# A written order for the first steps of an attention and MoE kernel, with three sums of the second product at once

## The chip, the cores and the metric

The kernel runs on one core of one Trainium2 chip. Its engines work side by side and wait for each other by semaphores: TensorE (PE) for matrix products, ScalarE (ACT), VectorE (DVE), GpSimd (POOL), and SyncE (SP), whose queue issues the loads. The metric is the time of one execution on the device in microseconds (us); lower is better.

## The reference

Attention at two resolutions for 2 batches and 8 heads of 576 positions with 64 dimensions, then two feed-forward blocks over the 1152 tokens:

```python
q_d, k_d, v_d = (means of 4 neighbouring positions of q, k, v)
out_up = np.repeat(softmax(q_d @ k_d.T * scale) @ v_d, 4, axis=2)
mask = np.abs(pos[:, None] - pos[None, :]) < 4
out_local = softmax(np.where(mask, q @ k.T * scale, -1e9)) @ v
x = (out_up + out_local)                      # tokens x 512
h = x @ w_in;  x = (h / (1 + np.exp(-h))) @ w_out        # 512 -> 2048 -> 512
p = domain_probs / (domain_probs.sum(-1, keepdims=True) + 1e-9)
out = sum(p[:, e:e+1] * (np.maximum(x @ w1[e], 0) @ w2[e]) for e in range(4))
```

## The kernel before

Products run as fp32r, each operand split in a high and a low part: high times high, high times low, low times high. So `mm3` (line 538) issues three matmuls for a product.

**Attention in jobs.** A job (line 494) is one batch, one pair of heads (`hp`) and one part `c` of the positions: 256 positions in four blocks of 64 for c = 0, 320 in five for c = 1. Jobs 0 to 3 are batch 0, c = 0; jobs 4 to 7 batch 0, c = 1; jobs 8 to 15 the same for batch 1 (the second batch). A job's steps are: `load_kq`, `load_vg`, `load_vw`; `local_scores` on PE (S below, 361); `local_max` on DVE (x, 378); `local_exp` on ACT (e, 385); pooled k and q (`pool_kq`, 314; for jobs 0 to 3 `pool_kq_first`, 328, where PE sums k with an identity); `down_scores` on PE (D, 392); `down_max` (n on DVE, d on ACT, 404); `local_sum` (u, 389); `norm` (r on DVE, g on ACT, 412); `trans` (T on PE, its evacuation a on ACT, 424); `values` (V on PE, o on ACT, f on DVE, 451); `split_x` (h on ACT, l on DVE, 473), which leaves the high and low part of the tokens in `xh`, `xl`. The last 64 positions of a batch's pooled scores are taken in one tail step (tp on POOL, tD and tT on PE).

**First feed-forward block.** Its 2048 columns are done in two halves (`hf`), each over four chunks of tokens (`ci`: 256, 320, 256, 320; in the second half 256, 256, 256, 384). Chunk 0 is jobs 0 to 3, chunk 1 jobs 4 to 7. For a chunk the first product (`g1_step`, 573; G below) makes eight blocks `ft` of 128 columns out of four `k`; `g1_evac` (556) makes x times sigmoid of it (th on ACT, gf on DVE) and splits it into `gh` (ACT) and `gl` (DVE). The second product (`g2_step`, 590; H below) sums over the eight blocks f for each of four blocks `db` of outputs. Of chunk 0 the first three blocks of G are summed job by job while the attention runs (`start_mm`, 828; M0 to M3). PSUM holds three tiles for these products (line 67).

**Weights.** They come as 64-bit pieces of 512 KB: pieces 0 to 7 are the first 1024 columns of w_in, 8 to 15 the matching rows of w_out. `split_raw` (197) turns a piece into a high part and a low part: two ACT steps (L208, L209; A below), one DVE step (L210; C), the copy to the high part on ACT (L217; w) and the low part on POOL (L218; L). Six pieces can be held (three `stg` buffers, three places in `acc`); their decoded form `dec` has two buffers.

**What sets the order.** The tile scheduler orders each engine by priorities, which `at_tick`, `attn_tick` and `prio` set, and by dependencies that `follow` adds within an engine without a semaphore. Each engine works through its list in order; on SP a load also waits until the load eight places before it has landed. `FIRST_LOADS` (120) sets the first loads by name.

Of the kernel before, what the change touches and what calls it, by code (L numbers as in the profile page):

```python
# [21 lines left out]
HP = NH // 2  # L22
# [34 lines left out]
STAGE = 4  # L57
EXPERT = 72
# [3 lines left out]
def attention_moe_kernel(ctx, tc, kqa, kqb, qtl, va, vb, w64, w1d, w2d, dpr, out):  # L62
# [57 lines left out]
    FIRST_LOADS = ("kq0", "kq1", "vg0", "vw0", "kq2", "vg1", "vw1", "kq3", "vg2", "vw2", "vg3", "vw3",  # L120
                   "s0", "s1", "s2", "s3", "kq4", "s4", "s5", "kq5")
# [75 lines left out]
    def split_raw(u, j, t):  # L197
# [3 lines left out]
        if u < 8:  # L201
# [10 lines left out]
            key = (u, j) if u < 2 else u  # L212
            if key in behind_job:
                for a in (first, low):
                    follow(a, behind_job[key][0], "first weights")
                follow(i, behind_job[key][1], "first weights")
            ACT.activation(out=h[:, c], in_=d, func=ACTF.Copy)  # L217
            POOL.tensor_tensor(out=l[:, c], in0=d, in1=h[:, c].bitcast(F32), op=ALU.subtract)  # L218
# [20 lines left out]
    def constants():  # L239
# [38 lines left out]
    def load_vw(j):  # L278
# [26 lines left out]
    def padd(o, a, b):  # L305
        POOL.tensor_tensor(out=o, in0=a, in1=b, op=ALU.add)  # L306
# [54 lines left out]
    def local_scores(j):  # L361
# [4 lines left out]
        for m in range(nb):  # L366
            for h in range(2):
# [5 lines left out]
                else:  # L373
                    after(i, first[h])
        j.group = PE.matmul(out=j.ps[:, 0:nb * WIN], lhsT=ident16, rhs=mk.rearrange("p m c -> p (m c)"),
                            start=False, stop=True, skip_group_check=True)

    def local_max(j):
# [3 lines left out]
        DVE.tensor_reduce(out=j.st[:, 0:nb], in_=j.lo, axis=AX.X, op=ALU.max)  # L382
        DVE.tensor_tensor(out=j.lo, in0=j.lo, in1=j.st[:, 0:nb].unsqueeze(2).to_broadcast([128, nb, WIN]), op=ALU.subtract)

    def local_exp(j):
        p = j.ps[:, 0:j.nb * WIN]
        ACT.activation(out=p, in_=p, func=ACTF.Exp, scale=SC_L)

    def local_sum(j):
        DVE.tensor_reduce(out=j.ps[:, 496:496 + j.nb], in_=j.lo, axis=AX.X, op=ALU.add)  # L390

    def down_scores(j):
        i = PE.matmul(out=j.ps[:, 352:352 + SD], lhsT=j.qd.rearrange("p a b -> p (a b)"), rhs=kd[j.b, j.hp],
                      start=True, stop=True)
        after(i, j.group)
# [631 lines left out]
```

## Time and profile before

| | |
|---|---|
| runs | 667.74, 667.77, 672.28 us; median 667.77 |
| profiled execution | 669.87 us; span from first to last instruction 667.6 us |
| busy in the span | PE 96%, DVE 63%, ACT 50%, POOL 37% |
| granted clock of PE, mean over the span | 0.986 |

A row of the busy table gives each engine's busy time in a stretch with its number of instructions. In the rows by time the first number is the start in us from the span's start, the second the time from the first start to the last end of the group, x the number of instructions; in brackets stands the idle time before and what ended it.

### The profile page before, as it was taken

The page shows a single profiled execution, that of the slowest core. Times are in us where ns is not written, and L with a number is a line of the kernel's source. Part 1 is how long each engine was busy: PE and PEld are TensorE (multiplying, and loading weights), DVE is VectorE, ACT ScalarE, POOL GpSimd, SP SyncE. Part 2 cuts the span into 40 slices and gives each one's busy share as a digit, 9 for nine tenths or more (in the row PEclk, how much of TensorE's full clock was granted, in tenths as well). Part 3 has the DMA queues.
Part 4 walks back from the last instruction along what each step waited for, and adds up shares of the span by engine and source line. Part 5 has one row for each costly group of instructions (what it writes and reads, how often), then busy time and mean ns, then how long its engine had stood idle before and what let it go on. Part 6 is the DMA issues. An engine that isn't in the chain of part 4 may idle for free.

```text
span 667.6 us, 13740 instructions
## 1 busy us (share of the span) xinstructions
PE 642.5 (96%) x5516; PEld 626.6 (94%) x5516; DVE 418.4 (63%) x851; ACT 330.5 (50%) x753; POOL 245.5 (37%) x346
## 2 busy tenths in 40 slices
PE   4879999999999999999999999999999999999995
PEld 4758988999999999999999999999999999999995
DVE  3569676475634644766467975568954769765444
ACT  2888765477843543454335643346533356433321
POOL 5546741114510000642356433456422654433210
PEclk9598999999999999999999999999999999999999
DMA  8975622007410400140002310012300020000001
GB/s 233 348 223 165 211 86 63 16 11 227 152 64 1 127 1 1 64 159 1 1 1 71 123 61 2 1 33 96 99 29 1 1 65 1 1 32 33 2 32 48
DMA packets 16927, 48.16 MB, mean 72 GB/s; under 512 B 2976, under 2 KB 4256, under 8 KB 16864
## 3 DMA queue, kind: packets, MB, share of 16 engines
q1 hardware_dynamic: 16864, 47.29, 22.3%
q8 instruction: 43, 0.70, 0.4%
q14 instruction: 20, 0.16, 0.1%
HBM read 44.93 MB, written 2.36 MB: 71 GB/s over the span
## 4 chain that ended last, share of the span: by engine, by line
PE 82%; DMA 6%; ACT 4%; DVE 4%; POOL 3%; issue 1%; SPq 0%; POOLq 0%; ACTq 0%; DVEq 0%
PE mm L540 52%; PE p L759 26%; DMA stg<-in_w_dram 3%; DMA vg<-in_va_dram 2%; DMA vg_f<-in_va_dram 1%; DVE gl L566 1%; DVE dec L210 1%; PE s L369 1%; ACT stg L209 1%; POOL wbuf L218 1%; PE t L432 1%; ACT dec L208 1%; PE o L464 1%; DVE acc L787 1%; POOL kq L306 1%
## 5 line engine op out<-in xcount | busy, mean ns | idle before, releaser
L540 PE MATMUL mm<-xh,wbuf 128*128 128x256 f32 (+2 forms) x1280 | 265.0, 294 | 5.4 <-DVE gf L560 3.5
L540 PEld LDWEIGHTS mm<-xh,wbuf 128*128 128x128 f32 x1280 | 208.9, 189 | 7.7 <-DVE gf L560 5.0
L540 PE MATMUL mm<-xl,wbuf 128*128 128x256 f32 (+2 forms) x640 | 187.7, 294 | 0.0
L741 POOL TENSOR_TENSOR r<-r 128x128 f32<-128x128 f32 x160 | 95.1, 607 | 177.8 <-ACT r L735 133.4
L744 DVE TENSOR_TENSOR h<-r,h 128x384 fp32r<-128x384 f32 (+1 forms) x128 | 91.8, 719 | 64.2 <-ACT h L743 64.0
L540 PEld LDWEIGHTS mm<-xl,wbuf 128*128 128x128 f32 x640 | 121.0, 189 | 0.2
L743 ACT ACTIVATE h<-r 128x384 fp32r<-128x384 f32 (+1 forms) x128 | 73.6, 578 | 93.3 <-POOL r L741 54.2
L540 PE MATMUL mm<-gh,wbuf 128*128 128x256 f32 (+2 forms) x512 | 102.6, 295 | 0.2 <-ACT acc L600 0.2
L759 PE MATMUL p<-wext,h 128*128 128x256 f32 x672 | 89.4, 276 | 0.0
L759 PE MATMUL p<-wbuf,h 128*128 128x256 f32 x672 | 82.7, 276 | 0.0
L540 PEld LDWEIGHTS mm<-gh,wbuf 128*128 128x128 f32 x512 | 81.9, 188 | 0.7 <-ACT acc L600 0.4
L759 PEld LDWEIGHTS p<-wext,h 128*128 128x128 f32 x672 | 82.4, 188 | 0.0
L759 PEld LDWEIGHTS p<-wbuf,h 128*128 128x128 f32 x672 | 79.4, 188 | 0.0
L540 PE MATMUL mm<-gl,wbuf 128*128 128x256 f32 (+2 forms) x256 | 74.0, 294 | 0.0
L741 DVE TENSOR_TENSOR r<-r 128x128 f32<-128x128 f32 x96 | 39.3, 409 | 35.6 <-ACT r L735 31.2
L735 ACT ACTIVATE r<-mm 128x512 f32<-128x512 f32 x48 | 28.6, 596 | 65.4 <-PE mm L540 65.0
L566 DVE TENSOR_TENSOR gl<-gf,gh 128x256 fp32r<-128x256 f32 (+2 forms) x64 | 39.0, 612 | 19.7 <-ACT gh L565 18.8
L540 PEld LDWEIGHTS mm<-gl,wbuf 128*128 128x128 f32 x256 | 47.8, 188 | 0.1
L218 POOL TENSOR_TENSOR wbuf<-dec,wbuf 128x512 fp32r<-128x512 f32 x24 | 32.1, 1354 | 25.9 <-ACT wbuf L217 19.8
L684 POOL TENSOR_TENSOR wext<-kst,wext 128x512 fp32r<-128x512 f32 x8 | 10.4, 1298 | 77.0 <-ACT wext L682 42.6
L560 DVE SCALAR_TENSOR_TENSOR gf<-th,mm 128x256 f32<-128x256 f32 (+2 forms) x64 | 28.4, 450 | 16.4 <-ACT th L559 15.1
L787 DVE SCALAR_TENSOR_TENSOR acc<-p,pr,acc 128x256 f32<-128x256 f32 (+1 forms) x63 | 36.1, 604 | 3.6 <-PE p L759 3.0
(138 smaller groups left out, 932.1 us busy)
## 6 DMA issues: line engine op xcount, KB each, us to landing
stg<-in_w_dram SPq DMA_DIRECT2D x25, 512.0 KB
kst<-in_w2d_dram SPq DMA_DIRECT2D x16, 512.0 KB
kst<-in_w1d_dram SPq DMA_DIRECT2D x12, 512.0 KB
acc<-in_w_dram SPq DMA_DIRECT2D x7, 512.0 KB
kq<-in_kqb_dram SPq DMA_DIRECT2D x8, 323.0 KB
kq<-in_kqa_dram SPq DMA_DIRECT2D x6, 419.0 KB
stg<-in_w1d_dram SPq DMA_DIRECT2D x4, 512.0 KB
vw<-in_vb_dram SPq DMA_DIRECT2D x8, 180.0 KB
```

The lines of the kernel that those rows point to most:

```text
L208: first = ACT.activation(out=d, in_=v[:, :, 1].bitcast(F32), func=ACTF.Prelu, scale=2.0 ** -112, alpha=2.0 ** 32)
L218: POOL.tensor_tensor(out=l[:, c], in0=d, in1=h[:, c].bitcast(F32), op=ALU.subtract)
L540: ins = [PE.matmul(out=ps, lhsT=l, rhs=r, start=(first and i == 0), stop=(last and i == n - 1)) for i, (l, r) in enumerate(pairs)]
L560: DVE.scalar_tensor_tensor(out=gf[:, 0:n], in0=th[:, 0:n], scalar=1.0, in1=ps[:, 0:n], op0=ALU.add, op1=ALU.mult)
L566: latest[DVE] = DVE.tensor_tensor(out=gl[ft][:, 0:n], in0=gf[:, 0:n], in1=gh[ft][:, 0:n].bitcast(F32), op=ALU.subtract)
L684: b = eng.tensor_tensor(out=l[:, r], in0=x, in1=h[:, r].bitcast(F32), op=ALU.subtract)
L735: ACT.activation(out=r[:, 0:4].rearrange("p s t -> p (s t)"), in_=ps[:, 0:512], func=ACTF.Relu)
L741: latest[eng] = eng.tensor_tensor(out=r[:, o], in0=r[:, a], in1=r[:, b], op=op)
L743: ACT.activation(out=h, in_=r[:, part], func=ACTF.Copy)
L744: latest[DVE] = DVE.tensor_tensor(out=l, in0=r[:, part], in1=h.bitcast(F32), op=ALU.subtract)
L759: ins = [PE.matmul(out=ps, lhsT=x, rhs=y, start=(opens and k == 0 and i == 0), stop=(k == 3 and i == n - 1), skip_group_check=True) for i, ...
L787: DVE.scalar_tensor_tensor(out=o, in0=ps, scalar=p, in1=o, op0=ALU.mult, op1=ALU.add)
```

## The change

The loads, and every step of the first eight jobs, of chunk 0 and of chunk 1's first product get a name by `mark`; the table `WRITTEN` lists the names engine by engine (one list each for SP, PE, ACT, DVE and POOL), and `written` ties each to the one before with `follow`. The ticks of jobs 0 to 3 stand closer. Other edits: k of jobs 0 to 3 is pooled by one DVE reduction in place of four PE products and an ACT copy; for pieces 0, 3, 9 and 13 the second of the two ACT steps is a shift on DVE (B below), for pieces 3 and 4 the copy to the high part is DVE's; `qdl` is zeroed by ACT at the start; in chunk 0 of the first half the second product runs three sums side by side, with f as the outer loop.

```diff
+LOW_ON_DVE = (0, 3, 9, 13)
+WHI_ON_DVE = (3, 4)
...
-    FIRST_LOADS = ("kq0", "kq1", "vg0", "vw0", "kq2", "vg1", "vw1", "kq3", "vg2", "vw2", "vg3", "vw3",
-                   "s0", "s1", "s2", "s3", "kq4", "s4", "s5", "kq5")
+    FIRST_LOADS = ("kq0", "kq1", "vg0", "vw0", "s0", "kq2", "vg1", "vw1", "s1", "kq3", "vw2", "vg2", "vg3", "s2",
+                   "vw3", "s3", "s4", "s5", "kq4", "s6", "vw4", "s7", "s8", "kq5", "s9", "qt", "vw5", "s10", "s11",
+                   "kq6", "s12", "kq7", "s13", "s14", "s15", "vw6", "vw7")
...
+    def mark(name, *ins):
+        steps.setdefault(name, []).extend(ins)
+        return ins[-1]
+
+    def written(names):
+        ins = [i for n in names.split() for i in steps[n]]
+        for a, i in zip(ins, ins[1:]):
+            follow(i, a, "written order")
...
-            low = ACT.activation(out=v[:, :, 0], in_=top, func=ACTF.Copy, scale=2.0 ** -13, bias=2.0 ** -14 - 0.5)
+            if 4 * u + j in LOW_ON_DVE:
+                low = mark(f"B{4 * u + j}", DVE.tensor_scalar(out=v[:, :, 0], in0=v[:, :, 0], scalar1=29, scalar2=None,
+                                                              op0=ALU.logical_shift_right))
+            else:
+                low = mark(f"A{4 * u + j}", ACT.activation(out=v[:, :, 0], in_=top, func=ACTF.Copy, scale=2.0 ** -13,
+                                                           bias=2.0 ** -14 - 0.5))
...
-            ACT.activation(out=h[:, c], in_=d, func=ACTF.Copy)
-            POOL.tensor_tensor(out=l[:, c], in0=d, in1=h[:, c].bitcast(F32), op=ALU.subtract)
+            if 4 * u + j in WHI_ON_DVE:
+                mark(f"w{4 * u + j}", DVE.tensor_copy(out=h[:, c], in_=d))
+            else:
+                mark(f"w{4 * u + j}", ACT.activation(out=h[:, c], in_=d, func=ACTF.Copy))
+            mark(f"L{4 * u + j}", POOL.tensor_tensor(out=l[:, c], in0=d, in1=h[:, c].bitcast(F32), op=ALU.subtract))
...
-        for r in range(4):
-            i = PE.matmul(out=kp, lhsT=ident, rhs=k4[:, :, r], start=(r == 0), stop=(r == 3))
-            if r == 0:
-                after(i, j.group)
-        ACT.activation(out=kd[j.b, j.hp], in_=kp, func=ACTF.Copy)
+        mark(f"k{j.i}", DVE.tensor_reduce(out=kd[j.b, j.hp], in_=k4, axis=AX.X, op=ALU.add))
...
-                    t = FIRST + PER * k
+                    t = FIRST + (PER if k > 3 else 2) * k
...
-    def g2_step(u0, hf, db, o, n):
+    def g2_step(u0, hf, dbs, o, n):
         c = slice(o, o + n)
-        ps = mm_tile()
+        sums = [(d, mm_tile()) for d in dbs]
         for f in range(8):
-            wh, wl = unit[u0 + f // 4]
...
+            for db, ps in sums:
+                g2_product(u0, db, f, ps, n)
+        for db, ps in sums:
+            g2_evac(hf, db, c, ps, n)
...
+    WRITTEN = (
+        """in_kq0 in_kq1 in_vg0 in_vw0 in_s0 in_kq2 in_vg1 in_vw1 in_s1 in_kq3 in_vw2 in_vg2 in_vg3 in_s2 in_vw3
...
+        """S0 S1 D0 D1 S2 T0 S3 T1 V0 D2 D3 V1 M0 T2 V2 M1 T3 S4 V3 M2 D4 S5 M3 tD G0_3_0 G0_3_1 D5 G0_3_2 G0_3_3
...
+        """tab e0 e1 A0 d0 d1 w0 g0 g1 A1 a0 w1 e2 e3 o0 a1 d2 h0 d3 A2 g2 o1 A3 h1 w2 a2 g3 A4 o2 A5 a3 h2 A6 e4
...
             for db in range(4):
                 next_step(dt)
-                g2_step(u0 + 2, hf, db, o, n)
+                if (hf, ci) != (0, 0):
+                    g2_step(u0 + 2, hf, [db], o, n)
+                elif db in (0, 3):
+                    g2_step(u0 + 2, hf, range(3) if db == 0 else range(3, 4), o, n)
```

The first loads on SP, at the program's start, in the kernel before (`stg` and `acc<-in_w` are pieces of weights, `kq` k and q of a job, `vg` and `vw` its v):

```order
L128 DMA kq<-in_kqa_dram 128x838 x2
L128 DMA vg_f_158<-in_va_dram 72x1024
L128 DMA vw<-in_va_dram 72x512
L128 DMA kq_f<-in_kqa_dram 128x838
L128 DMA vg_f_200<-in_va_dram 72x1024
L128 DMA vw<-in_va_dram 72x512
L128 DMA acc<-in_kqa_dram 128x838
L128 DMA vg_f_279<-in_va_dram 72x1024
L128 DMA vw_f_284<-in_va_dram 72x512
L128 DMA vg_f_376<-in_va_dram 72x1024
L128 DMA vw_f_381<-in_va_dram 72x512
L128 DMA stg_135<-in_w_dram 128x512
```

The same place in the changed kernel:

```order
L131 DMA kq<-in_kqa_dram 128x838 x2
L131 DMA vg_f_156<-in_va_dram 72x1024
L131 DMA vw<-in_va_dram 72x512
L131 DMA stg_137<-in_w_dram 128x512
L131 DMA kq_f<-in_kqa_dram 128x838
L131 DMA vg_f_186<-in_va_dram 72x1024
L131 DMA vw<-in_va_dram 72x512
L131 DMA stg_231<-in_w_dram 128x512
L131 DMA acc<-in_kqa_dram 128x838
```

The first piece of weights has moved from behind the loads of four jobs to the fifth place, the second to the ninth.

ACT's first steps before (`dec<-stg` and `stg<-stg` are A, `wbuf<-dec` is w, `kd<-s` the copy of pooled k, `s<-s` e, `ed,s<-` d, `ed<-ed` g, `at` and `atd` a):

```order
L336 ACTIVATE kd<-s 128x144
L387 ACTIVATE s<-s 128x280
L336 ACTIVATE kd<-s 128x144
L387 ACTIVATE s<-s 128x280
L409 ACTIVATE ed,s<-s,st 128x144 x2
L420 ACTIVATE ed<-ed,st 128x144
L208 ACTIVATE dec<-stg_135 128x512
L209 ACTIVATE stg_135<-stg_135 128x512
L208 ACTIVATE dec<-stg_211 128x512
L209 ACTIVATE stg_211<-stg_211 128x512
L420 ACTIVATE ed<-ed,st 128x144
```

And in the changed kernel:

```order
L410 ACTIVATE s<-s 128x280 x2
L222 ACTIVATE dec<-stg_137 128x512
L433 ACTIVATE ed,s<-s,st 128x144 x2
L239 ACTIVATE wbuf<-dec 128x512
L445 ACTIVATE ed<-ed,st 128x144 x2
L222 ACTIVATE dec<-stg_231 128x512
L228 ACTIVATE stg_231<-stg_231 128x512
L458 ACTIVATE at<-t_233 70x512
L465 ACTIVATE atd_243<-t_234 72x256
L239 ACTIVATE wbuf<-dec 128x512
```

The first two pieces now stand among the exponentials and scalings of jobs 0 and 1, and the copies of pooled k are gone.

On PE, the second product of chunk 0 where the middle blocks of f are used, in the changed kernel (`gh_642` and `gl_641` are f = 2, `gh_640` and `gl_639` f = 3; o is V of job 6):

```order
L565 MATMUL mm<-gh_642,wbuf 128x256 x2
L565 MATMUL mm<-gl_641,wbuf 128x256
L565 MATMUL mm<-gh_642,wbuf 128x256
L565 MATMUL mm<-gh_640,wbuf 128x256
L565 MATMUL mm<-gl_639,wbuf 128x256
L565 MATMUL mm<-gh_640,wbuf 128x256
L483 MATMUL o<-atd_587,vd 64x80 x4
L487 MATMUL o<-at,vw 64x64 x10
L565 MATMUL mm<-gh_640,wbuf 128x256
L565 MATMUL mm<-gl_639,wbuf 128x256
```

Each f is used by three sums before the next f; before, the scheduler put four or five f of one sum in a row.

## Rows read from the trace of the kernel before

**Rows 1.** The page's first part: busy us (share of the span) and instructions.
```profile
PE 642.5 (96%) x5516; PEld 626.6 (94%) x5516; DVE 418.4 (63%) x851; ACT 330.5 (50%) x753; POOL 245.5 (37%) x346
```

**Rows 2.** Busy time by stretches: stretch, its length, engines; granted clock, DMA share.
```profile
core 0: us, PE busy (x) PEld busy (x) DVE busy (x) ACT busy (x) POOL busy (x), PEclk, DMA share, GB/s
20.00:25.00 5.00, 4.12 (x47) 2.83 (x44) 3.01 (x6) 4.95 (x11) 0.84 (x1) 0.50 1.03 407
...
20.00:75.00 55.00, 48.42 (x523) 41.74 (x520) 42.30 (x100) 48.68 (x126) 29.90 (x37) 0.87 0.70 235
...
85.00:667.60 582.60, 573.76 (x4810) 566.74 (x4808) 365.27 (x721) 270.75 (x599) 198.03 (x273) 1.00 0.15 48
```

**Rows 3.** TensorE in order of time: start us, us, [idle before <-releaser].
```profile
31.31 0.61 PE L540 MATMUL mm<-xh,wbuf 128*128 128x256 f32 x3
...
50.60 0.38 PE L540 MATMUL mm<-xh,wbuf 128*128 128x256 f32 x1 [2.77 <-DVE gf L560]
...
82.67 0.50 PE L460 MATMUL o<-atd,vd 72*64 72x80 f32 x8
82.96 0.79 PE L464 MATMUL o<-at,vw 70*64 70x64 f32 x20
```

**Rows 4.** Loads issued on SP, and ACT's first step on weights, by time.
```profile
8.35 0.30 SPq L128 DMA_DIRECT2D vw_f<-in_va_dram  x1
...
9.84 0.35 SPq L128 DMA_DIRECT2D stg<-in_w_dram  x1
...
12.09 0.33 SPq L128 DMA_DIRECT2D stg<-in_w_dram  x1
...
19.45 0.66 ACT L208 ACTIVATE dec<-stg 128x512 f32<-128x512 f32 x1 [1.61 <-DMA stg<-in_w_dram]
```

**Rows 5.** TensorE at a granted clock of 0.50: transposes, then scores.
```profile
18.33 1.06 PE L432 MATMUL t<-ident,sm 128*70 128x128 f32 x4
...
20.80 1.20 PE L369 MATMUL s<-acc 64*64 64x70 f32 x16
```

**Rows 6.** ACT in order of time: an interval between two starts prices the first.
```profile
39.25 0.59 ACT L435 ACTIVATE at<-t 70x512 f32<-70x512 f32 x1 [0.39 <-PE t L432]
39.74 0.37 ACT L442 ACTIVATE atd<-t 72x256 f32<-72x256 f32 x1
40.01 0.38 ACT L476 ACTIVATE xh<-o 128x256 fp32r<-128x256 f32 x1
40.27 1.26 ACT L208 ACTIVATE dec<-stg 128x512 f32<-128x512 f32 x2
41.44 1.23 ACT L209 ACTIVATE stg<-stg 128x512 int32<-128x512 uint16 x2
42.56 0.37 ACT L409 ACTIVATE ed<-s,st 128x144 f32<-128x144 f32 x1
...
43.40 1.15 ACT L217 ACTIVATE wbuf<-dec 128x512 fp32r<-128x512 f32 x2
44.44 0.38 ACT L476 ACTIVATE xh<-o 128x256 fp32r<-128x256 f32 x1
```

**Rows 7.** VectorE and GpSimd in order of time, by start.
```profile
32.03 1.31 DVE L210 SCALAR_TENSOR_TENSOR dec<-dec,acc 128x512 int32<-128x512 int32 x2
...
53.13 3.54 DVE L566 TENSOR_TENSOR gl<-gf,gh 128x256 fp32r<-128x256 f32 x2
...
53.30 2.52 POOL L218 TENSOR_TENSOR wbuf<-dec,wbuf 128x512 fp32r<-128x512 f32 x2
```

**Rows 8.** TensorE in order of time, full clock: scores of the second batch, products.
```profile
70.54 0.71 PE L369 MATMUL s<-kq 64*64 64x70 f32 x16
...
72.28 0.39 PE L540 MATMUL mm<-gh,wbuf 128*128 128x256 f32 x1
...
78.53 0.39 PE L540 MATMUL mm<-gh,wbuf 128*128 128x256 f32 x2
...
80.91 0.41 PE L393 MATMUL s<-kd,qbd 128*128 128x144 f32 x2
```

More of the change, by code (lines that the diff above doesn't have):

```diff
@@ L208, in split_raw @@
             first = ACT.activation(out=d, in_=v[:, :, 1].bitcast(F32), func=ACTF.Prelu, scale=2.0 ** -112, alpha=2.0 ** 32)
-            low = ACT.activation(out=v[:, :, 0], in_=top, func=ACTF.Copy, scale=2.0 ** -13, bias=2.0 ** -14 - 0.5)
+            mark(f"A{4 * u + j}", first)
+            if 4 * u + j in LOW_ON_DVE:
[4 more added lines that the diff above has]
+                                                           bias=2.0 ** -14 - 0.5))
             i = DVE.scalar_tensor_tensor(out=ai, in0=ai, scalar=3, in1=v[:, :, 0],
                                          op0=ALU.logical_shift_left, op1=ALU.bitwise_or)
[L212 to L216, printed above, removed]
-            ACT.activation(out=h[:, c], in_=d, func=ACTF.Copy)
-            POOL.tensor_tensor(out=l[:, c], in0=d, in1=h[:, c].bitcast(F32), op=ALU.subtract)
+            mark(f"C{4 * u + j}", i)
+            if 4 * u + j == 16:
+                for a, b in ((first, "gh0_7"), (low, "gh0_7"), (i, "gl0_7")):
+                    follow(a, steps[b][-1], "written order")
+            if 4 * u + j in WHI_ON_DVE:
[3 more added lines that the diff above has]
+            mark(f"L{4 * u + j}", POOL.tensor_tensor(out=l[:, c], in0=d, in1=h[:, c].bitcast(F32), op=ALU.subtract))
         else:
@@ L252, in constants @@
             POOL.memset(t, 0.0)
-        POOL.memset(qdl, 0.0)
+        z = ac.tile([128, 1], F32, name="zero")
+        DVE.memset(z, 0.0)
+        mark("tab", ACT.activation(out=qdl.rearrange("p a b c -> p (a b c)"), in_=z.to_broadcast([128, HP * 32]), func=ACTF.Copy))
     class Job:
-        pass
+        i = None
     kd, vd, atd = {}, {}, {}
@@ L285, in load_vw @@
         else:
-            last_load.append(SP.dma_start(out=j.vw, in_=vb[j.b, j.hp]))
+            last_load.append(load(f"vw{j.i}", j.vw, vb[j.b, j.hp]))
     def load_vg(j):
@@ L305, in padd @@
     def padd(o, a, b):
-        POOL.tensor_tensor(out=o, in0=a, in1=b, op=ALU.add)
+        return POOL.tensor_tensor(out=o, in0=a, in1=b, op=ALU.add)
     def pmul(o, a, b):
@@ L340, in pool_kq_first @@
             p = slice(64 * h, 64 * h + 64)
-            DVE.tensor_reduce(out=j.qd[p, h], in_=q4[p], axis=AX.X, op=ALU.add)
+            mark(f"q{j.i}", DVE.tensor_reduce(out=j.qd[p, h], in_=q4[p], axis=AX.X, op=ALU.add))
     def pool_v(j):
@@ L414, in norm @@
         sums = j.ps[:, 496:497 + nb]
-        DVE.tensor_scalar(out=sums, in0=sums, scalar1=1e-9, scalar2=None, op0=ALU.add)
-        DVE.reciprocal(out=j.st[:, 13:14 + nb], in_=sums)
+        mark(f"r{j.i}", DVE.tensor_scalar(out=sums, in0=sums, scalar1=1e-9, scalar2=None, op0=ALU.add),
+             DVE.reciprocal(out=j.st[:, 13:14 + nb], in_=sums))
         if nb:
@@ L419, in norm @@
             i = DVE.tensor_tensor(out=j.sm, in0=j.lo, in1=j.st[:, 13:13 + nb].unsqueeze(2).to_broadcast([128, nb, WIN]), op=ALU.mult)
-        a = ACT.activation(out=j.ed, in_=j.ed, func=ACTF.Copy, scale=j.st[:, 13 + nb:14 + nb])
-        if nb and j.i < 2:
-            behind_job.update({(0, 2 * j.i): (a, i), (0, 2 * j.i + 1): (a, i)})
+            mark(f"r{j.i}", i)
+        mark(f"g{j.i}", ACT.activation(out=j.ed, in_=j.ed, func=ACTF.Copy, scale=j.st[:, 13 + nb:14 + nb]))
     def trans(j):
@@ L441, in trans @@
             dst = j.atd
-        ACT.activation(out=dst, in_=t2[0:72, 1:3].rearrange("p a (h q) -> p a h q", h=2), func=ACTF.Copy)
+        mark(f"a{j.i}", ACT.activation(out=dst, in_=t2[0:72, 1:3].rearrange("p a (h q) -> p a h q", h=2), func=ACTF.Copy))
     def tail_trans(l):
@@ L898, in attention_moe_kernel @@
             if hf == 0 and ci == 2:
+                for names in WRITTEN:
+                    written(names)
                 close_attn()
```

137 lines of the change are left out of this document (86 added, 51 removed).

## The prediction

> **What bounds the kernel now.** I read the page first, then the busy time by stretches, then the engines' rows in order of time. TensorE is busy for 642.5 us of the 667.6 us span [rows 1], so all that can be won is in its idle time and in stretches at the low clock. From 85 us on it is busy for 573.76 of 582.60 us at a granted clock of 1.00 [rows 2]; the other 25.1 − 8.8 = 16.3 us of idle time lie before 85 us. The reader should see in [rows 2] that between 20 and 75 us the granted clock is 0.87 and that ScalarE (ACT) is busy for 48.68 of 55 us: no other engine is that full there. The marks of the start are in [rows 3]: the first product with weights at 31.31, the fourth block of chunk 0 only at 50.60, after 2.77 us of waiting for VectorE's `gf` (it frees the PSUM tile), and the values of job 7, among chunk 1's first products, from 82.67 to 82.96 + 0.79 = 83.75. From there on TensorE hardly waits. So the time is set by how soon TensorE has done the first eight jobs and both products of chunk 0. I take the end of job 7's values as the mark: 83.75 us, less some 0.3 for a product and a pooled score that had slipped ahead of it, 83.4.
>
> Why is that late? ACT has hardly anything to do until the first weights land and it reads them at 19.45 [rows 4]; it then has all sixteen pieces, eight jobs and chunk 0's evacuations in one queue.
>
> **The change, part by part.**
>
> *Order of the loads.* Transfers stream one behind the other: SP's rows start when the transfer eight places before has landed, so a whole k/q takes 9.84 − 8.35 = 1.49 us and a pair of pooled and windowed v 12.09 − 9.84 = 2.25 [rows 4]; a piece of weights 524 KB / 407 GB/s = 1.29 [rows 2]. Before, the first weights stood behind all twelve loads of four jobs. Now the first piece stands behind kq0, kq1, vg0 and vw0, which had landed by 8.35 [rows 4]: 8.35 + 1.29 = 9.6 us, some 10 us sooner. Then kq2 (1.49), vg1 and vw1 (2.25), the second piece (1.29) and kq3 (1.49): kq3 lands at 16.1, two pieces later than before. The fourth piece comes when it came before, since the same bytes stand ahead of it. So weights do not come sooner on the whole; two of them fill ACT's idle time.
>
> *Work off TensorE and ACT.* The sums of k for jobs 0 to 3 leave TensorE, and four copies of them leave ACT; VectorE does them in one reduction each. No row has this shape; two reductions of 256 elements or the longest row of a job bound it between 0.5 and 1.0 us, I take 0.8. TensorE's share costs nothing now where it waited anyway. Four low-bit steps leave ACT (1.12 / 2 = 0.56 each [rows 6]) and two weight copies (0.52 each), 3.3 us in all. On VectorE no row shows either form. Above, each is bounded by the row with two inputs of the same width, 1.31 / 2 = 0.66 [rows 7]; below by half of that, if one input streams twice as fast; I take 0.6, the row nearest in width. The zeroing of `qdl` and the table load move to ACT's idle start and are hidden.
>
> *The order of the chain to the first product.* TensorE's rows are S2 T0 S3 T1 V0 D2 D3 V1 M0 T2. I assume the clock of 0.50 that [rows 5] were run at, since TensorE is as thinly used in this stretch as before. S3 starts when kq3 lands, 16.1, and takes 1.20 + 0.4: 17.7. T1 takes 1.06 + 0.43 = 1.5: 19.2. V0 at half clock is twice job 7's 1.08 less the end's overlap [rows 3], 2.1: 21.3. Scale, add, high part and low part go over ACT and VectorE, with other steps between: an estimate of 2.4 from four dependent steps of some 0.4 us and two others: 23.7. M0 is nine products at twice 0.113 [rows 8], 2.0: 25.7, against 31.31 before. T2, 1.5, and its evacuation on ACT, 40.01 − 39.25 = 0.76 [rows 6]: 28.0. There ACT takes up the fifth piece (A4).
>
> *ACT's queue from A4 to the last copy of weights.* Prices are intervals between rows [rows 6]: ten pieces with both steps, (42.56 − 40.27) / 2 = 1.14 each, 11.4; two with the first alone, 0.58 each, 1.2; eleven copies at 1.04 / 2 = 0.52, 5.7; eight tanh at 0.26 (as a high part, 40.27 − 40.01) and eight `gh`, taken at 0.05 more, 4.6; the exponentials, pooled exponentials and scalings of jobs 4 to 7 (0.84 for one of each: 43.40 − 42.56), 3.8; evacuations of the transposes, 3.9; high parts and normalizations, ten at about 0.3, 3.1. Together 33.7 us. ACT will also wait. I take the share that it waited before in its full stretch, 55 / 48.68 = 1.13 [rows 2]: 38.1 us, of which 4.4 is waiting. So the last copy is done at 28.0 + 38.1 = 66.1.
>
> *Behind it.* GpSimd's last two low parts take 2.52 / 2 = 1.26 each [rows 7], the first of them under the last copy: 1.5 us, 67.6. TensorE then still has the last f of three sums and all of the fourth, 33 products at (80.91 − 78.53) / 21 = 0.113, 3.7; scores of jobs 8 and 9, 72.28 − 70.54 = 1.74 [rows 8]; values of job 7, 1.05. That is 6.5 us: the mark falls at 74.1.
>
> *Three sums at once.* With f outside, a piece of w_out serves three blocks when it lands, and what is left behind the last piece is one f of each, not a whole sum. Before, the scheduler had already mixed the blocks, so I book nothing for it beyond the 6.5 above. Its cost: three sums hold all three PSUM tiles, so the fourth waits for the first evacuation (about 0.4 on ACT, free by then); hidden by the scores of jobs 8 and 9 that stand there.
>
> *The sum.* 83.4 − 74.1 = 9.3 us sooner; everything behind the mark keeps its work. The profiled execution took 669.87 us (667.6 of it span), so it would take 660.6; it lies 2.1 above the median of the runs. From the median, 667.77 − 9.3 = **658.5 us**.
>
> **Strictness, and what is late next.** An order by hand lets one late step hold a queue. Two places are worth watching. VectorE's shift of piece 13 stands ahead of job 5's normalization, and on SP that piece stands behind kq7, which waits for GpSimd's sums of job 5. And TensorE's tail scores stand ahead of the fourth block, behind GpSimd's tail sums; these come at about 38 us by the same prices, the PSUM tile at about the same time.
>
> **The rivals.**
>
> *VectorE becomes the bound.* It was busy 42.30 of 55 us [rows 2]; four shifts and two copies at 0.6 make it 46 of the 54 us from 20 to 74.1. [rows 7] show two `gl` of VectorE taking 3.54 us where GpSimd ran two low parts of 2.52 just then, while two steps of 0.66 ran undisturbed at 32.03. Some 26 steps with both inputs in SBUF (or of the new forms) stand in the stretch; GpSimd is busy 29.90 of 55 us; a mean wait of half of 1.26 makes 26 × 0.54 × 0.63 = 8.8 us, against 8 us of slack, of which I think half can be used: 4.7 us lost, mark at 78.8, 663.2 us. The Trainium skill, "SBUF — State Buffer", section "Who interferes with whom", says that a VectorE step with two SBUF inputs, or a copy or tensor_scalar in a two-port mode, and a GpSimd step that reads SBUF shut each other out for a whole instruction. By that rule the new shifts and copies would join the waiting; the trace agrees for `gl`, and no row of before shows the new forms.
>
> *ACT waits for nothing.* The order was written so that each step finds its input: 28.0 + 33.7 + 1.5 + 6.5 = 69.7, 13.7 us won, 654.1 us. Against it: steps pass between four engines, and two buffers of `dec` tie each piece to GpSimd's low part two pieces before.
>
> *Given back later.* The second batch now starts its scores inside the second product and stands later among chunk 1's products. Three or four waits like the one that [rows 3] show at 50.60 would cost up to 8 us, one or two of them 2.8 to 5.5: about 662 to 664.
>
> *Slower.* Piece 13: every microsecond that it lands after VectorE reaches its shift (about 45 us) falls on the mark. Before, the longest way from issue to use in a busy queue was 19.45 − 9.84 = 9.6 us [rows 4]; issued at about 41 it lands by 51 at the latest on that scale, a loss of 6 us, not enough. Slower by over 1% needs it (or another first-in-line) 9.3 + 6.7 = 16 us late, landing at 61. I see nothing that would do it.
>
> That the order isn't what is written is excluded: the built rows stand as the table says.
>
> **How the numbers follow.** The forecast has 0.55 (its own range 655 to 661), ACT without waits 0.15, VectorE as bound 0.20, given back 0.06, slower 0.04. One per cent, about what a measurement of this kernel can tell from no change, is 6.7 us: faster means under 661.1. So faster 0.55 + 0.15 = 0.70, same 0.26, slower 0.04. The range leaves out the best tail of the case without waits and the slower cases: 652 (the chain to A4 at full clock saves a further 2 us) to 665 (VectorE as bound with somewhat more of the 8.8 us).
>
> **What would show it.** First piece read near 9.7 us; first product with weights near 24 to 26; ACT over 0.88 busy from 28 to 66; the last copy of weights near 66 and the mark near 74; behind it the same work as before, with idle time within 1 us of the 8.8. VectorE `gl` rows over 1 us, or shifts over 0.7, speak for the first rival. Wrong would be: a mark after 79, or a mark near 74 with a total above 662.

## The result and the profile after

The changed kernel takes 660.39 us (median of 4 runs, 658.84 to 661.81) beside 669.03 for the kernel before in the same set; the ratio is 0.9856, 95% interval 0.9825 to 0.9888, which is 7.5 to 11.7 us. In a later set it was 661.73 beside 670.89, ratio 0.9883 (0.9847 to 0.9918). The forecast was 658.5 in a range of 652 to 665, 9.3 us under the 667.77 from which it started; the medians above lie 8.6 us apart, over the one per cent that the prediction calls faster (0.70). Kernels compared below take 0.5% more or less from one execution to the next. They were timed in four sets, with before at 669.03 (after), 669.70 (no_order, low_on_act, two_sums, tail_fixed), 670.89 (after_again, tail_again, early_only, k_on_pe) and 671.44 (the other four). One kernel, timed in the second set as tail_fixed and in the third as tail_again, has medians of 665.79 and 662.50. So a difference of 2 us within a set, or of 3 us between sets, says nothing; the marks below come from one execution each. The profiled execution of tail_fixed took 678.22 us, and what is longer in it lies behind chunk 1's start (597.7 us there, 581.9 in after), so only its marks are used.

The page of after and busy time by stretches, the lines that answer to [rows 1, 2] (columns as there):

```profile
PE 630.2 (96%) x5484; PEld 616.3 (94%) x5484; DVE 418.8 (64%) x862; ACT 327.6 (50%) x744; POOL 245.3 (37%) x345
```

```profile
20.00:25.00 5.00, 3.15 (x46) 2.83 (x41) 4.23 (x15) 4.52 (x14) 2.46 (x4) 1.00 1.00 341
20.00:75.00 55.00, 45.45 (x555) 40.00 (x550) 42.09 (x104) 47.21 (x122) 32.39 (x42) 0.97 0.77 245
85.00:657.70 572.70, 564.12 (x4758) 558.30 (x4757) 356.77 (x704) 266.10 (x587) 199.28 (x275) 1.00 0.16 48
```

The same view cut at the first product of chunk 1, which comes at 82.31 us before and at 75.82 after; first the two lines of before, then those of after:

```profile
0.00:82.31 82.31, 66.13 (x670) 57.45 (x671) 52.27 (x128) 58.20 (x149) 47.49 (x73) 0.90 0.74 235
82.31:667.60 585.29, 576.40 (x4848) 569.12 (x4846) 366.13 (x724) 272.31 (x604) 198.03 (x273) 1.00 0.16 49
```

```profile
0.00:75.82 75.82, 56.87 (x664) 48.78 (x665) 56.36 (x140) 56.34 (x142) 43.92 (x68) 0.98 0.81 250
75.82:657.70 581.88, 573.30 (x4822) 567.48 (x4820) 362.40 (x723) 271.26 (x602) 201.33 (x278) 1.00 0.16 50
```

TensorE's idle time in the start did not shrink: 82.31 − 66.13 = 16.2 us before, 75.82 − 56.87 = 18.9 after. Its busy time did, by 9.3 us, although after has job 7's values (1.05) in it too. Two things left it: the sums of k, which took 4.45, 2.40 and 2.24 us of TensorE in the timeline of before, 9.1 together; and some 1.2 us more, put down to time at the low rate (below), which no run separates. The lines of before for the sums:

```profile
8.99 4.45 PE L333 MATMUL s<-kq,ident 128*128 128x144 f32 x16 [1.15 <-DVE s L383]
...
25.26 2.40 PE L333 MATMUL s<-kq_f,ident 128*128 128x144 f32 x8
...
29.08 2.24 PE L333 MATMUL s<-acc,ident 128*128 128x144 f32 x8
```

TensorE of after in order of time, the rows that answer to [rows 3, 5, 8]:

```profile
13.64 1.20 PE L389 MATMUL s<-kq_f 64*64 64x70 f32 x16 [3.64 <-DVE s L439]
...
16.92 1.20 PE L389 MATMUL s<-acc 64*64 64x70 f32 x16 [0.46 <-DVE dec L230]
...
18.26 0.80 PE L455 MATMUL t<-ident,sm 128*70 128x128 f32 x4
...
22.68 0.46 PE L483 MATMUL o<-atd,vd 72*64 72x64 f32 x8 [1.85 <-POOL vd L330]
22.93 0.67 PE L487 MATMUL o<-at,vw 70*64 70x64 f32 x16
23.53 0.38 PE L565 MATMUL mm<-xh,wbuf 128*128 128x256 f32 x1
...
38.79 0.45 PE L424 MATMUL s<-kd,qdl 128*32 128x144 f32 x8 [1.22 <-DVE s L405]
39.68 0.38 PE L565 MATMUL mm<-xh,wbuf 128*128 128x256 f32 x1 [0.43 <-DVE gf L586]
...
53.00 0.48 PE L416 MATMUL s<-kd,qbd 128*128 128x144 f32 x2 [1.47 <-ACT s L410]
...
67.01 0.41 PE L457 MATMUL t<-ident,ed 128*72 128x128 f32 x2 [0.77 <-ACT ed L445]
...
69.50 0.71 PE L389 MATMUL s<-kq 64*64 64x70 f32 x16
...
72.97 0.76 PE L487 MATMUL o<-at,vw 70*64 70x64 f32 x20
...
75.82 0.30 PE L565 MATMUL mm<-xh,wbuf 128*128 128x320 f32 x1
```

The first product with weights comes at 23.53 where it came at 31.31, the fourth block at 39.68 instead of 50.60, and the 2.77 us wait for `gf` has become 0.43, with 1.22 more ahead of the tail scores, which stand before that block in the written row. Job 7's values end at 72.97 + 0.76 = 73.73, but the last eighteen products of the fourth sum now stand behind them; with the same work done, the mark of the prediction (83.4 before) is the first product of chunk 1, 75.8.

ScalarE of after, the last pieces (L222 and L228 are a piece's two steps, L239 its copy), and GpSimd's last two low parts:

```profile
61.35 0.69 ACT L222 ACTIVATE dec<-stg 128x512 f32<-128x512 f32 x1
61.91 1.31 ACT L228 ACTIVATE stg<-stg 128x512 int32<-128x512 uint16 x2
63.10 0.68 ACT L222 ACTIVATE dec<-acc 128x512 f32<-128x512 f32 x1
63.66 0.67 ACT L228 ACTIVATE acc<-acc 128x512 int32<-128x512 uint16 x1
65.34 0.68 ACT L228 ACTIVATE stg<-stg 128x512 int32<-128x512 uint16 x1 [1.01 <-DMA stg<-in_w_dram]
65.92 0.61 ACT L239 ACTIVATE wbuf<-dec 128x512 fp32r<-128x512 f32 x1
...
66.86 0.62 ACT L239 ACTIVATE wbuf<-dec 128x512 fp32r<-128x512 f32 x1
```

```profile
66.61 2.53 POOL L240 TENSOR_TENSOR wbuf<-dec,wbuf 128x512 fp32r<-128x512 f32 x2 [4.65 <-ACT wbuf L239]
```

Pieces 14 and 15 have three steps L228 between 61.91 and 64.3 where two are theirs, and a fourth at 65.34 waits 1.01 us for a load: two low-part steps of pieces 16 and 17 stand ahead of the copy of piece 14. The table does not name them; only piece 16 is tied, behind `gh0_7`.

### The profile page after: what moved, and what is told of

The parts are those of the page before. It is cut to its first block, busy times and chain, and to the rows that moved or that the text cites. A ratio compares the mean times of both kernels' runs of the same rounds, so it can differ in the third digit from the quotient of the medians.

```text
span 657.7 us, 13693 instructions
## 1 busy us (share of the span) xinstructions
PE 630.2 (96%) x5484; PEld 616.3 (94%) x5484; DVE 418.8 (64%) x862; ACT 327.6 (50%) x744; POOL 245.3 (37%) x345
## 4 chain that ended last, share of the span: by engine, by line
PE 79%; DMA 11%; DVE 3%; ACT 3%; POOL 2%; issue 1%; SPq 0%; ACTq 0%; POOLq 0%; DVEq 0%
PE mm L565 50%; PE p L794 26%; DMA stg<-in_w_dram 4%; DMA vg<-in_va_dram 2%; DMA acc<-in_kqa_dram 2%; DMA acc<-in_w_dram 2%; DMA qt<-in_qtl_dram 1%; DVE dec L230 1%; ACT stg L228 1%; PE t L455 1%; POOL vg L330 1%; ACT dec L222 1%; DMA kq<-in_kqa_dram 1%; PE o L487 1%; DVE acc L822 1%
## 5 line engine op out<-in xcount | busy, mean ns | idle before, releaser
L565 PE MATMUL mm<-gl,wbuf 128*128 128x256 f32 (+2 forms) x256 | 74.1, 292 | 0.0
L592 DVE TENSOR_TENSOR gl<-gf,gh 128x256 fp32r<-128x256 f32 (+2 forms) x64 | 34.6, 543 | 17.9 <-ACT gh L591 17.5
L591 ACT ACTIVATE gh<-gf 128x256 fp32r<-128x256 f32 (+2 forms) x64 | 28.1, 442 | 21.6 <-DVE gf L586 20.7
```

What stands on the lines that cost most here:

```text
L565: ins = [PE.matmul(out=ps, lhsT=l, rhs=r, start=(first and i == 0), stop=(last and i == n - 1)) for i, (l, r) in enumerate(pairs)]
L591: latest[ACT] = mark(f"gh{c}_{ft}", ACT.activation(out=gh[ft][:, 0:n], in_=gf[:, 0:n], func=ACTF.Copy))
L592: latest[DVE] = mark(f"gl{c}_{ft}", DVE.tensor_tensor(out=gl[ft][:, 0:n], in0=gf[:, 0:n], in1=gh[ft][:, 0:n].bitcast(F32), op=ALU.subtract))
```

## The experiments

The table holds each kernel's ratio to before and, from its one profiled execution, the starts of the first product with weights (M), of the first product of the second kind (gh), the end of the last weight copy (w15), the start of chunk 1 (c1), and the stretches in which TensorE's rows have the length of the low rate.

| kernel | ratio (95%) | M | gh | w15 | c1 | low rate, us |
|---|---|---|---|---|---|---|
| before | 1 | 31.3 | 64.9 | 73.3 | 82.3 | 4.0–31, 51–54 |
| after | 0.9856 (0.9825–0.9888) | 23.5 | 55.1 | 67.5 | 75.8 | 4.2–18.5, 29–32 |
| after_again | 0.9883 (0.9847–0.9918) | 22.9 | 54.4 | 66.7 | 75.0 | 4.3–17.6, 28–31 |
| no_order | 1.0042 (1.0016–1.0069) | 30.3 | 68.0 | 60.6 | 87.9 | 4.2–53.7 |
| low_on_act | 0.9896 (0.9847–0.9945) | 25.1 | 60.6 | 73.0 | 81.3 | 4.2–19.8, 24–33, 44–47 |
| two_sums | 0.9950 (0.9928–0.9972) | 23.0 | 56.5 | 67.8 | 78.5 | 4.1–17.4, 28–31, 41–44 |
| tail_fixed | 0.9925 (0.9895–0.9955) | 27.8 | 59.3 | 69.4 | 78.5 | 4.0–29.8, 44–47 |
| tail_again | 0.9890 (0.9860–0.9919) | 23.9 | 57.2 | 67.7 | 76.7 | 4.0–18.4, 22–32, 56–60 |
| early_only | 1.0008 (0.9981–1.0035) | 30.4 | 63.4 | 72.5 | 81.5 | 4.3–30, 50–53 |
| k_on_pe | 1.0059 (1.0032–1.0086) | 38.1 | 69.6 | 80.8 | 89.2 | 4.3–40.6, 54–58 |
| late_loads | 0.9933 (0.9908–0.9959) | 24.6 | 60.6 | 72.7 | 81.1 | 4.4–19.6, 23–37 |
| thin_low | 0.9819 (0.9779–0.9859) | 22.7 | 53.4 | 64.9 | 72.8 | 4.4–16.8, 27–30 |
| tail_and_exp | 0.9887 (0.9853–0.9920) | 27.3 | 57.9 | 68.2 | 77.7 | 4.2–30.5, 81–85 |
| k_on_dve_only | 1.0106 (1.0058–1.0155) | 26.5 | 67.3 | 72.6 | 93.1 | 4.2–20.8, 28–41.5, 50–55, 86–89 |

> The changed kernel once more, beside the others of this set, so that they stand against runs of the same hour. Both theories: 660 to 662, chunk 1 begins near 75.8.

It came in as expected; two executions of one kernel differ by 0.8 us in c1.

**The written order.**

```diff
-                for names in WRITTEN:
-                    written(names)
```

> The changed kernel without the order by hand: the tie that puts each engine's first steps into the written rows is left out, and the scheduler places them; the earlier loads, the sums of k on VectorE, the shifts and copies on VectorE and three sums at once stay. Theory A (the written order carries the gain): chunk 1 begins near 82, as in the kernel before, median 666 to 670. Rival B (moving work off TensorE and the two early pieces carry it, whatever the order): chunk 1 begins near 76 to 77, median 660 to 662.

All other edits without the order are not faster than before: 672.67 us beside 669.70, with c1 at 87.9 in the profiled execution. The gain is gone, as in theory A and beyond what it gave. ScalarE has all sixteen weights done at 60.6, 7 us sooner than in after, and chunk 0 comes later: weights alone are not what TensorE waits for. But there is a second thing in the trace, a busy-time line and TensorE rows of this kernel:

```profile
45.00:50.00 5.00, 5.00 (x41) 4.59 (x40) 4.96 (x11) 3.73 (x10) 4.05 (x4) 1.00 0.86 319
```

```profile
46.32 0.63 PE L565 MATMUL mm<-xh,wbuf 128*128 128x256 f32 x2
46.75 0.41 PE L565 MATMUL mm<-xl,wbuf 128*128 128x256 f32 x1
46.96 0.63 PE L565 MATMUL mm<-xh,wbuf 128*128 128x256 f32 x2
...
57.60 0.40 PE L565 MATMUL mm<-xh,wbuf 128*128 128x256 f32 x2
57.83 0.28 PE L565 MATMUL mm<-xl,wbuf 128*128 128x256 f32 x1
57.95 0.39 PE L565 MATMUL mm<-xh,wbuf 128*128 128x256 f32 x2
```

Three products take 46.96 − 46.32 = 0.64 us there, 0.35 at 57.6. Up to 53.7 every row has the low rate's length, though the granted clock's column says 1.00. From M to 53.7 that is some 23 us, mostly busy; at the full rate they would be about half, and c1 near 77 if TensorE alone set it, by that estimate from this one trace. How much of the order's worth is its rows and how much the earlier rise to the full rate, these runs do not separate.

**The sums of k.** Back on TensorE in the written order, and alone in the kernel before:

```diff
-        mark(f"k{j.i}", DVE.tensor_reduce(out=kd[j.b, j.hp], in_=k4, ...))
+        for r in range(4):
+            PE.matmul(out=kp, lhsT=ident, rhs=k4[:, :, r], ...)
+        mark(f"k{j.i}", ACT.activation(out=kd[j.b, j.hp], in_=kp, ...))
```

> The changed kernel with the sums of k for jobs 0 to 3 back on TensorE and their copies on ScalarE, in the written order right behind each job's scores. Theory A (TensorE waits there anyway, as the prediction booked it: nothing): chunk 1 begins within 1 us of the changed kernel. Rival B (the chain to the first product pays for them): each job costs four products and a copy of 0.4 us, some 1 us, on the chain of jobs 0, 2 and 3; the first product with weights and chunk 1 come 2 to 4 us later, median 662.5 to 664.5.

> The kernel before with one edit: the sums of k of jobs 0 to 3 by one reduction each on VectorE; the rest, its scheduler's order too, follows from that. Theory A (the sums of k, 9.1 us of TensorE's time in the kernel before, are the larger part of the gain, in any order): the first product with weights comes 4 us or more earlier than 31.3, chunk 1 begins near 77 to 78, median 662 to 664. Rival B (they need the written order): chunk 1 begins at 80 to 83, median 666 to 670.

TensorE's rows of k_on_pe:

```profile
7.35 2.40 PE L356 MATMUL s<-kq,ident 128*128 128x144 f32 x8 [1.45 <-DVE s L411]
...
12.25 2.40 PE L356 MATMUL s<-kq,ident 128*128 128x144 f32 x8 [1.03 <-DVE s L411]
...
22.59 2.40 PE L356 MATMUL s<-kq_f,ident 128*128 128x144 f32 x8 [1.10 <-DVE s L411]
...
28.63 2.29 PE L356 MATMUL s<-acc,ident 128*128 128x144 f32 x8 [1.04 <-DVE s L411]
```

Rival B, and far above its 2 to 4 us: four sums of 2.3 to 2.4 and four waits of 1.0 to 1.5 make 9.5 + 4.6 = 14.1 us on a strict queue, M comes 14.5 us later, and the kernel is no faster than before (674.82 beside 670.89). The sums and the chain behind them run at the low rate here, up to 40.6 us, which is in these figures. Alone, without the order, the same edit brings M forward by 4.8 us, but c1 comes 10.8 us later: in its trace (an execution of 681.45 us, median 676.94) TensorE waits 3.28 us ahead of 50 and for 1.6 to 2.1 us at four other places, and the low rate comes back three times. Of theory A only the earlier M came, and neither theory's c1. So neither the written order with the sums on TensorE nor the scheduler's order with the sums on VectorE is faster than before; they win together.

**The early loads.** In the kernel before, and taken back in after:

```diff
-FIRST_LOADS = ("kq0", "kq1", "vg0", "vw0", "kq2", "vg1", "vw1", "kq3", ..., "vw3", "s0", "s1", ...
+FIRST_LOADS = ("kq0", "kq1", "vg0", "vw0", "s0", "kq2", "vg1", "vw1", "s1", "kq3", ...
```

> The kernel before with one edit: the first two pieces of weights are loaded where the changed kernel loads them; every engine's order stays that of before. Theory A (the earlier loads are worth nothing without the written order, since in the order of before ScalarE has nothing that it could do sooner but two pieces): ScalarE reads the first piece near 13 and not 19.45, chunk 1 begins within 1.5 us of 82.3, median 667 to 670. Rival B (the earlier loads carry much of the gain): chunk 1 begins 4 us or more earlier, median under 665.

> The changed kernel with the loads in the order of before (all twelve of four jobs ahead of the first weights); ScalarE's, VectorE's and GpSimd's steps for the first two pieces are written further behind, so that no queue stands before a load that is not there. Theory A (two early pieces fill ScalarE's idle start, as the prediction put it): two pieces' steps of 1.1 and copies of 0.5, some 3.3 us, fall into its full stretch; chunk 1 begins 2.5 to 4 us later than the 75.0 to 75.8 of the changed kernel. Rival B (the early loads are worth nothing here either, as in early_only, since the chain of the first jobs sets the first product): within 1 us, and the first product with weights not later than 24.

Alone they are worth nothing (c1 0.8 us earlier, ratio 1.0008): ScalarE read the first piece at 17.80, not near 13: job 0's normalization stands ahead of it in that order and starts only at 17.48. In the written order they are worth some 3 to 4 us: late_loads is at 665.83 (ratio 0.9933; after_again has 0.9883, and tail_and_exp, of the same set, 662.00), its c1 at 81.1, its M only 1 to 1.6 us later. Theory A in kind; the low clock in its trace from 23 to 37 us is part of the 5 to 6 us at c1.

**VectorE's shifts and copies.**

```diff
-LOW_ON_DVE = (0, 3, 9, 13)
-WHI_ON_DVE = (3, 4)
+LOW_ON_DVE = ()
+WHI_ON_DVE = ()
```

> The changed kernel with its four shifts and two weight copies back on ScalarE, at the same places of the written order. Theory A (ScalarE's queue sets the end of the start, as the prediction booked it): 3.3 us of steps and waiting in proportion, so the last weight copy and the start of chunk 1 come 3.3 to 3.7 us later, median near 664. Rival B (ScalarE has slack, TensorE or the loads set the end): within 1 us of the changed kernel, 660 to 661.

Busy time from the fifth piece's start to the last copy, low_on_act and then after:

```profile
29.34:72.97 43.63, 36.75 (x408) 32.50 (x409) 30.79 (x73) 37.52 (x97) 21.31 (x27) 0.91 0.68 219
```

```profile
27.15:67.48 40.33, 34.27 (x408) 30.29 (x409) 32.37 (x77) 35.86 (x92) 21.37 (x27) 0.96 0.80 247
```

It takes 43.6 us there, in after 40.3. That this is the 3.3 us of theory A is chance: of the six steps the shifts of pieces 0 and 3 lie ahead of this stretch, and the four in it are 2.2 us by the prediction's prices. ScalarE is busy for only 1.7 us more and idle for 1.6 more, with waits of 1.39 and 1.38 for GpSimd's low parts and one of 1.65 for TensorE, at the low rate just then. The fifth piece also starts 2.2 us later, and c1 comes 5.5 us later, more than theory A's 3.7, in an execution that is at the low rate from 24 to 33 and 44 to 47 us. The total, 663.70 of four runs from 661.25 to 666.24, is as theory A says (664), but its interval overlaps that of after. So the steps cost ScalarE time, and how much of it reaches the total is not shown.

**Three sums at once.**

```diff
-H0_0_0 H0_1_0 D7 T6 V5 H0_2_0 H0_0_1 H0_1_1 H0_2_1 ... H0_0_7 H0_1_7 H0_2_7
+H0_0_0 H0_1_0 D7 T6 V5 H0_0_1 H0_1_1 ... H0_0_7 H0_1_7 H0_2_0 H0_2_1 ... H0_2_7
```

> The changed kernel with the second product of chunk 0 in another order: two sums side by side, then the third whole, then the fourth, so 54 products stand behind the last low part of the weights and not 33. Theory A (three sums at once saves nothing of its own, as the prediction booked it, because TensorE is as full either way): within 1 us of the changed kernel. Rival B (what is left behind the last low part sets the end): 21 products at 0.113 us, 2.4 us later, median near 662.8.

Rival B: from the last copy to c1 it takes 10.7 us (78.48 − 67.77), in the two executions of after 8.3 and 8.4, so 2.4 us more, as 21 products at 0.113 us give; the last copy itself comes when it does in after (67.8). What stands behind the last low part is the price. The medians, 666.72 here and 661.73 in after_again, are of different sets; tail_fixed, of the same set, has 665.79, so the total does not show the price.

**The two steps ahead of the copy, and one wait of TensorE.** tail_fixed and tail_again are one kernel; in tail_and_exp ScalarE's `e6` also stands ahead of `A12`.

```diff
-            if 4 * u + j == 16:
-                for a, b in ((first, "gh0_7"), (low, "gh0_7"), (i, "gl0_7")):
+            if 16 <= 4 * u + j < 20:
+                for a, b in ((first, "w15"), (low, "w15"), (i, "gl0_7")):
```

> The changed kernel with the steps of pieces 16 and 17 (second weight set) placed behind the last weight copy of piece 15 on ScalarE. In the changed kernel two of their low-part steps stand ahead of the copy of piece 14 there: one of 0.58 us, and one that waits 1.01 us for its load and takes 0.58. Theory A (ScalarE's queue sets the mark): copies and last low part 2.2 us earlier (67.0 where it was 69.1), chunk 1 begins near 73.6, median 2.2 lower. Rival B (TensorE has no more than the 0.77 us of idle time at 67.0 to give): chunk 1 begins near 75.0, 0.8 us lower.

> The kernel of tail_fixed again, whose profiled execution was 13 us longer than its others. Theory A (ScalarE's queue sets the mark): from the fifth piece's start to the last weight copy 2.2 us less than in the changed kernel (40.3 there), chunk 1 begins 2 us earlier, near 73.7. Rival B (TensorE has only 0.77 us of idle time to give): 0.8 us earlier, near 75.0.

> The kernel of tail_fixed with one step more: ScalarE's exponential of job 6 stands ahead of the twelfth piece's two steps and not behind them; TensorE's pooled scores of job 6 wait for it 1.47 us in the changed kernel. Theory A (TensorE's idle time between 39 and 68 us can be taken away step by step): 1.2 us from this, 1.2 us from the other, chunk 1 begins near 73, median 2 to 2.5 us under the changed kernel's. Rival B (what one wait gives back another takes, since ScalarE's queue is as long as before): chunk 1 within 1 us of 75.0 to 75.8.

The executions started differently (M from 23.9 to 27.8, with nothing changed ahead of it), and no c1 lies ahead of after's, so stretches are compared. From the fifth piece's start to the last copy, which the second expectation names, it takes 40.3 us in both executions of after and 37.7, 39.5 and 36.6 here: 2.6 less and, for the same kernel, 0.8 (with the low rate from 22 to 32 us), then 3.7. Nearer to the steps, from gh to w15, it takes 12.3 us in both executions of after, and 10.1, 10.6 and 10.2 here: 1.7 to 2.2 less, close to theory A. From gh to c1 it takes 20.7 and 20.6 in after, and 19.2, 19.5 and 19.8: only 0.9 to 1.5, near rival B (some of tail_again's low stretch at 56 to 60 us lies in its 19.5). TensorE's idle time there is 1.5 us in both executions of after and 0.7, 0 and 0.9 here, so there was no more than 1.5 to win. The one step more acts ahead of gh: from M to gh it takes 30.6 us in tail_and_exp, 31.5 in tail_fixed and 31.6 and 31.5 in after, 0.9 less in one execution. TensorE's waits around it, in tail_and_exp:

```profile
54.90 0.48 PE L416 MATMUL s<-kd,qbd 128*128 128x144 f32 x2 [0.35 <-ACT s L410]
56.21 0.50 PE L483 MATMUL o<-atd,vd 72*64 72x80 f32 x8 [0.82 <-ACT atd L471]
...
59.81 0.71 PE L455 MATMUL t<-ident,sm 128*70 128x128 f32 x5 [0.68 <-DVE sm L443]
```

The wait of 1.47 is down to 0.35, and one of 0.82 has come up behind it. None of the totals shows a gain: tail_again's 662.50 stands beside after_again's 661.73 in one set, tail_and_exp has 662.00 (ratio 0.9887, after_again 0.9883), tail_fixed 665.79.

**GpSimd's low parts.**

```diff
-            mark(f"L{4 * u + j}", POOL.tensor_tensor(out=l[:, c], in0=d, ...))
+            e = slice(c.start, c.start + (64 if u < 4 else 512))
+            mark(f"L{4 * u + j}", POOL.tensor_tensor(out=l[:, e], in0=d[:, 0:e.stop - e.start], ...))
...
+        wl = wh if u0 < 4 else wl
```

> The changed kernel with GpSimd's low parts of the first weight set cut to 64 of 512 columns; the products of that set read the high part in place of the low part, in as many products as before. This leaves out most of the low parts' values and nothing of TensorE's work. Theory A (VectorE's waiting beside GpSimd costs little): chunk 1 begins within 1.5 us of the changed kernel, 74 to 75.8. Rival B (the prediction's first rival: VectorE loses 4.7 us to GpSimd's low parts): 70.5 to 71.5.

Between the two: c1 at 72.8, 2.2 to 3.0 us earlier than in the executions of after, the median 658.60 (ratio 0.9819, after_again 0.9883). The products no longer wait for a low part either, so this bounds what VectorE's waiting is worth at c1 from above, in one execution. The second low part (`gl`) of chunk 0 on VectorE in after, and GpSimd beside it; then the same step in thin_low:

```profile
43.01 1.50 DVE L592 TENSOR_TENSOR gl<-gf,gh 128x256 fp32r<-128x256 f32 x1
```

```profile
41.71 2.53 POOL L240 TENSOR_TENSOR wbuf<-dec,wbuf 128x512 fp32r<-128x512 f32 x2 [1.73 <-ACT wbuf L239]
```

```profile
41.57 0.42 DVE L594 TENSOR_TENSOR gl<-gf,gh 128x256 fp32r<-128x256 f32 x1
```

## Why the prediction was right, and where it was not

**What bounds the kernel.** "All that can be won is in its idle time and in stretches at the low clock" was wrong. Ahead of chunk 1 the idle time grew by 2.8 us, and TensorE's busy time fell by 9.3; 9.1 us of work left it, a third place which the prediction had read (its step on k) and priced at nothing. Taken off alone, this work gave no gain (k_on_dve_only).

**The first piece and the chain.** The first piece was read at 9.22 (9.6 to 9.7 forecast). T1 ended at 18.89 + 0.38 = 19.3 (19.2; S3 had started 0.8 us late, and T1 was shorter by nearly as much), the first product came at 23.53 (23.7), the fifth piece at 27.15 (28.0). The agreement is partly luck. The low rate was right up to 18.5 (S2 and S3 still take 1.20) and wrong behind it: V0 and M0 ran at the full rate, three products in 0.35 us, and gave back some 2 us. In exchange S2 waited 3.64 us for VectorE, and V0's hand-over took 3.4 and not 2.4, with 1.85 us of waiting ahead of V1.

**k on VectorE.** One reduction takes 0.75 us (0.8). That TensorE's share costs nothing is the step that failed: k_on_pe puts 14.5 us on it in the written order. It did not spoil the sum, as the chain was worked out without the sums of k.

**ScalarE's queue.** From the fifth piece to the last copy 40.3 us, forecast 38.1. ScalarE is busy for 35.9 us there (33.7) and idle for 4.5 (4.4). The count of steps left out the two low-part steps of pieces 16 and 17, 1.2 us of work, and 1.01 of waiting for the second one's load. These two make the 2.2 us that the forecast is short of, but not alone: the other steps took 1.0 more than booked and the other waits 0.9 less, which cancel. One booked term has no row: four times 0.84 is 3.4 and not 3.8, and the 0.84 of [rows 6] holds a normalization's step (L467) and no scaling. Taking the two steps away shortened the stretch by 2.6 us in one execution and 0.8 in another. Busy from 28 to 66 us ScalarE was 33.5 of 38, the 0.88 that was named as a sign. The shift and the copy take 0.42 to 0.43 each (0.6; bounds 0.33 to 0.66); the 3.3 us that they were to take off ScalarE are not shown as such (low_on_act).

**Behind it.** The last low part ended at 69.14 (67.6); the remainder took 75.82 − 69.14 = 6.7 (6.5). The mark fell at 75.8, in the other execution at 75.0 (74.1): 7.6 to 8.4 us sooner, not 9.3. The rest of the gain lies behind the mark: span 657.7 against 667.6 is 9.9, so 2.3 of it; in after_again 0.9. Idle time there was 8.58 us, as forecast; the rest is a slightly shorter busy time for the same products, which differs between executions of one kernel, and nothing here ties it to the change.

**Three sums.** Booked at nothing beyond the remainder of 6.5 us, which has them in it. Against two sums side by side they are worth 2.4 us behind the last copy (two_sums); against the mixed order of before no run shows their worth.

**The rivals.** VectorE as the bound was there with a smaller size: at most 2.2 to 3.0 us, with the last low part's own tail in it, for 4.7. Two `gl` took 1.50 us for 0.42 where GpSimd's low parts ran, the sign that was named for it. The Trainium skill, "SBUF — State Buffer", section "Who interferes with whom", has such a VectorE step shut out by a GpSimd step that reads SBUF; the trace agrees. The new shifts and copies are shut out too, as the prediction took from that page. In after none of them lay beside a low part for longer than 0.11 us, but a shift in no_order took 0.91 us for 0.42 and a copy in two_sums 0.65, and each ended 0.28 us after the low part beside it, as the two pairs of lines show. So in after they stayed clear by when they ran, and not by their form.

```profile
36.05 1.27 POOL L240 TENSOR_TENSOR wbuf<-dec,wbuf 128x512 fp32r<-128x512 f32 x1 [0.52 <-ACT wbuf L239]
...
36.69 0.91 DVE L225 TENSOR_SCALAR acc<-acc 128x512 int32<-128x512 int32 x1
```

```profile
26.32 1.27 POOL L240 TENSOR_TENSOR wbuf<-dec,wbuf 128x512 fp32r<-128x512 f32 x1 [3.51 <-DVE s L439]
...
27.22 0.65 DVE L237 CAST wbuf<-dec 128x512 fp32r<-128x512 f32 x1
```

"ACT waits for nothing" did not come (ScalarE is busy 47.21 of 55 us). "Given back later" did not come either. Piece 13 was no hindrance: its shift ran at 46.06 without a wait. The tail scores, the other place that the prediction watched, held TensorE for 1.22 us.

## What to carry to other kernels

An order written by hand is worth what its slowest queue allows: cost what it takes off each strict queue as well as what it adds, since a step in a written row (a sum of 2.4 us on TensorE) costs its whole length and its wait. Count in a queue's sum every step that the new order does not name, too. And compare a start at the rate that its rows show, not at the rate of the column, before an edit is given the credit.

## What the hardware showed unexpectedly

TensorE's first rows have the low rate's length with a granted clock of 1.00 in the column: scores of 1.20 us at 4.2 and 13.64 in after, as at 0.50 in [rows 5]. The column falls to 0.50 in other stretches, in after only from 29 to 32 us. The rows' rise to the full rate comes at 18.5 us in after, at 31 before, at 40.6 in k_on_pe and at 53.7 in no_order. In after TensorE had run from 16.92 without a gap when they rose; in no_order it was busy for 5.00 of 5 us in three stretches from 35 us on and they did not rise until 53.7. The Trainium skill, "TensorE: Matmul & The Clock Gate", Part 1, says that the clock is low by default and activity releases it; the first rise in after agrees, and the long wait in no_order is not explained by these runs.

The start also differs between executions of the same order, along with the speed of the loads: at 294 to 310 GB/s from 5 to 25 us (after, after_again, tail_again) the first product came at 22.9 to 23.9 and the rise at 17.6 to 18.5; at 273 to 279 (tail_fixed, tail_and_exp, the same orders up to there) they came at 27.3 to 27.8 and near 30. The speed alone does not give it: low_on_act, with 278 GB/s, has its first product at 25.1 and the rise at 19.8. What causes what is open.
